# Spectral block with a gated MLP: the second token block transposed by VectorE and DMA, where TensorE did it

## The chip, the core and the metric

The kernel runs on one core of a Trainium2 chip. The core has five engines with queues of their own, which run in order and wait for each other by semaphores: TensorE (PE in the profile; its weight loads are PEld), VectorE (DVE), ScalarE (ACT), GpSimd (POOL) and SyncE (SP), which here issues nearly all DMAs. TensorE writes to PSUM, eight banks of 128 partitions x 2 KB; the other tensors lie in SBUF, 128 partitions wide. The metric is the device time of one execution in microseconds, the median of three runs.

## The reference

```python
x = A_x                                                  # 1 x 2048 tokens x 640 features, float32
X = rfft2(layernorm(x)) * (w_r + 1j * w_i)
h = x + irfft2(X)
n = layernorm(h)
out = h + ((n @ w_gate) * (n @ w_up)) @ w_down           # 640 -> 1728 -> 640
```

## The kernel before

The first part, up to about 180 us, does the Fourier filter as matrix products and adds its result to x; from there on the tiles X[0] to X[15] hold h, 128 tokens x 640 features each. The rest is the gated MLP, in two blocks of 1024 tokens (blk 0: X[0..7], blk 1: X[8..15]); a block has two halves sb of 512 tokens.

Products need n transposed, features on the partitions. The tile xt[:, sb, k, l] holds, for half sb and feature block k of five, 128 features x 512 tokens, split in a high part (l = 0, rounded to the fast product type) and a low part (l = 1, what is left). Every product is done as three matmuls, high x high, high x low and low x high.

Hidden features come in 14 chunks of 128. Chunks 12 and 13 are made by plain products, gate and up (gu), and multiplied by gate_parts. Chunks 0 to 11 go through strassen: gate and up, feature blocks 0-1 and 2-3 and the two token halves make a 2 x 2 block product, done by the Winograd form in six steps with seven product groups (the fifth feature block is added to them). The form needs sums of n's blocks: t1 = n(1, k) - n(0, k), t2 = n(1, k+2) - t1, t3 = t2 - n(0, k) and t4 = n(0, k+2) - t2, each split in high and low as well; t4 takes the place of xt[:, 1, 0:2]. The chunks go in pairs p; the order of the pairs in a block is 6, 0, 1, 2, 3, 4, 5, where 6 stands for chunks 12 and 13. A pair's down products are done during the next pair, by groups that strassen starts at its slots 1 to 7 (at(n)): slots for the even chunk and slots for the odd one. Into the same slots the lists side put other work. The last pair's down products, one per token tile (down), stand at the change of blocks: 12 matmuls into two of four PSUM banks (tag d), then two additions to X on VectorE and the tile's store.

Everything is emitted in the order in which the program is written, and each engine's queue follows it. What sets the work around the change:

- prep(c): the weights of chunk c lie raw in stage; ScalarE and GpSimd split them (copies), form the weights' own sums (sums) and split those (high, low). load_raw then loads the next chunk's into stage, on SP's queue.
- The pool work has eight buffers (wk) for everything short-lived: ScalarE's copies h0, c22 and h1 of each chunk, of which an even chunk's are kept until the odd one, the raw down weights (draw), normalised tiles. A new tile takes a buffer that is free, and its first writer waits for the old one's last reader, a DMA too.
- fill holds the 32 small operations that make the layernorm factors of X[8..15]; one is popped behind each group of down products, the rest at chunk 11.
- At the end of block 0 (chunk 11) ScalarE normalises X[8..15] (L646), and TensorE starts to transpose them: turn_mm makes four 128 x 128 transposes of one token tile into a PSUM bank of tag e (L658), turn_hi copies them to xt and, for tiles 0 to 3, to bt, turn_lo makes the low part and, for tiles 4 to 7, the first two sums (L681, L682). fifth does the fifth feature block of four tiles at once (L689). These alternate with the eight down products. Behind them stand the plain products gu of chunks 13 and 12, and beside them t12, t_rest and t34 finish the sums.

Of the kernel before, what the change touches and what calls it, by code (L numbers as in the profile page):

```python
# [16 lines left out]
P = 128  # L17
# [4 lines left out]
NC = 14  # L22
# [16 lines left out]
def f32(ap):  # L39
    return ap.bitcast(F32)  # L40
# [29 lines left out]
def tile_spectral_glu(ctx: ExitStack, tc: tile.TileContext, x, wf, wgu, wlast, wdown, wdlast,  # L70
# [595 lines left out]
    def turn_hi(t):  # L666
        hi, pk = turned(t, 0)
        act(hi, pk, AF.Copy)
        if t % 8 == 0:
            TJ["b"] = home("dA", [P, 4, 4, P], "bt")  # L670
        if t % 8 < 4:
            act(TJ["b"][:, t % 4], pk[:, 0:4], AF.Copy)

    def turn_lo(t):
        lo, pk = turned(t, 1)
# [39 lines left out]
    def transp(t):  # L715
        turn_mm(t)
        turn_hi(t)
        turn_lo(t)
# [228 lines left out]
    def strassen(c, blk, ahead, downs, side):  # L947
# [84 lines left out]
        elif odd:  # L1032
            hi_of(oa, 5)
            lo_of(oa, 5)

    order = [6, 0, 1, 2, 3, 4, 5]
    steps = [(blk, p) for blk in range(2) for p in order]
    prev = None
    for n, (blk, p) in enumerate(steps):
        if p == 6:  # L1040
            if blk == 0:
                load_raw(0)
                copies, sums, high, low = prep(0, blk, nc.vector)
# [24 lines left out]
                wdn = load_d(p)  # L1068
            else:
                copies, sums, high, low = prep(0, blk)  # L1070
                js = [4, 5, 6, 7, 0, 1, 2, 3]
                for j in range(8):
                    if j:
                        transp(8 + j)
                    else:
                        turn_lo(8)
                    if j % 4 == 3:
                        fifth(range(5 + j, 9 + j))
                    if j >= 1:
                        down(*prev, js[j - 1], True)  # L1080
                    if j == 3:
                        copies()
                        sums()
                    if j == 5:
                        high()
                        low()
                down(*prev, js[7], True)
                wdn = load_d(p)
                gu(NC - 1, 0)
                gate_parts(NC - 1, 0)()  # L1090
                gu(NC - 2, 0)
                TJ["12"] = home("qr", [P, 2, 2, 2, 512], "t12", F32R)
                t1s = [t12(j) for j in range(4)]
                late = gate_parts(NC - 2, 0)
                for j in range(4):
                    t1s[j][0]()
                    t_rest(j)
                late()
                gu(NC - 1, 1)
                for j in range(4):  # L1100
                    t1s[j][1]()
                late = gate_parts(NC - 1, 1)
                issue(wdn)
                hi, lo = t34(0)
                hi()
                late()
            gu(NC - 2, 1)
            g = gate_parts(NC - 2, 1, wdn[0] if blk == 0 else ())
            rest = t34(1)
            rest[0]()  # L1110
            g()
            lo()
            rest[1]()
# [12 lines left out]
        if prev[1] == 6:  # L1126
            js = [[0], [1, 2], [3], [4, 5], [6, 7]]
            slots[0] = {n: [lambda j=j, prev=prev: down(*prev, j) for j in k] for n, k in enumerate(js, 3)}
        else:
            fs = down_products(*prev, (0, 1)) + down_products(*prev, (2, 3))  # L1130
            slots[0] = dict(zip(range(1, 8), fs))
            slots[1] = dict(zip((1, 2, 7) if p == 5 else (2, 3, 4), fs[7:]))
        for ci in range(2):
            c = 2 * p + ci
            side = {n: [] for n in range(8)}
            ahead = None
            if c < 11:
                ahead = prep(c + 1, blk)
                if c < 10:
                    side[6 if ci else 7].append(lambda c=c: load_raw(c + 2))  # L1140
            if p == 5:
                if ci == 0:
                    side[3].append(lambda wdn=wdn: issue(wdn))
                else:
                    side[4].append(lambda: (split(HELD["a11"], 0), split(HELD["a21"], 3)))
            elif ci == 0:
                for n, i in ((3, 0), (6, 1), (7, 2)):
                    side[n].append(wdn[i])
            else:
                def rest(wdn=wdn, ahead=ahead):  # L1150
                    split(HELD["a11"], 0)
                    ahead[2]()
                    ahead[3]()
                    wdn[3]()
                    split(HELD["s3"], 5)
                    wdn[4]()

                side[4].append(rest)
            if c == 11 and blk == 0:
                pop(len(fill))  # L1160
                dj = load_direct(1, [wk([P, D], "draw"), stage[:, 0:640], stage[:, 640:1280]])
                side[1] += [lambda: issue(dj[0]), lambda: issue(dj[1]), lambda: load_raw(0)]

                def norms(ks):
                    for k in ks:
                        if k == 0:
                            TJ["z"] = home("qr", [P, 6, D], "zt")
                        normalise(8 + k, TJ["z"][:, k] if k < 6 else wk([P, D], "z"))

                for n, ks in ((3, (0, 1, 2)), (5, (3, 4)), (6, (5, 6)), (7, (7,))):  # L1170
                    side[n].append(lambda ks=ks: norms(ks))
                side[7] += [lambda: turn_mm(8), lambda: turn_hi(8)]
            strassen(c, blk, ahead, slots[ci], side)
        prev = (blk, p)
    for j in (4, 5, 6, 0, 1, 2, 3, 7):
# [132 lines left out]
```

## Time and profile before

| | |
|---|---|
| median of 3 runs | 691.53 us (691.51 to 691.61) |
| the profiled execution | 692.1 us |
| its span in the trace | 690.3 us |
| TensorE busy, share of the span | 98% |
| VectorE, ScalarE, GpSimd | 69%, 46%, 56% |
| chunks 8 to 11 of block 0 | about 336 to 411 us of the span |
| down products and transposes at the change of blocks | 411 to 430 us |
| the four plain products behind them | 430 to 450 us |

A row of the timeline has the start and the length in us, the engine, the line, the operation, what it writes and reads, the shape, a count where equal instructions follow each other, and in brackets how long the engine stood idle before it and what released it. A row of the groups has the count, the busy time, the mean ns of one, and the idle time before them. PE's matmuls are pipelined: the pace is read from the starts, best of the weight loads. A row of a DMA queue has its packets, its MB and the time that they took as a share of 16 engines' span; a row of DMA issues has the count, the size of one and the median us from issue to landing.

### The profile page before, as it was taken

How to read it: one execution, taken by the hardware profiler on the slowest of the kernel's cores; microseconds unless marked ns; L12 is line 12 of the kernel's file. 1: busy time of each engine (PE TensorE's matmuls, PEld its weight loads, DVE VectorE, ACT ScalarE, POOL GpSimd, SP SyncE). 2: the span in 40 equal slices, each digit the busy share in tenths (PEclk: the TensorE clock that was granted, in tenths of full speed). 3: DMA queues.
4: the chain of work that ended last, by engine and by line, in shares of the span. 5: the costliest groups of instructions: out<-in, count | busy, mean ns of one | idle time of the engine just before them, and what ended most of it. 6: DMA issues, size and time to landing. Idle time of an engine off the chain costs nothing.

```text
span 690.3 us, 10276 instructions
## 1 busy us (share of the span) xinstructions
PE 679.8 (98%) x3784; PEld 602.3 (87%) x3784; DVE 478.3 (69%) x980; ACT 318.8 (46%) x615; POOL 383.4 (56%) x364
## 2 busy tenths in 40 slices
PE   8999999999999999999999999999999999999998
PEld 8989998887888888888888889888888888888887
DVE  7968887897963858586867648553757575765654
ACT  6976665375533434252525184342625252525320
POOL 3101113321097887878787644086887878797610
PEclk9999999999999999999999999999999999999999
DMA  9516763001120212121212112401212121212004
GB/s 334 195 56 213 236 206 118 1 1 38 43 78 35 76 39 77 39 76 39 77 38 96 39 39 114 153 1 38 78 39 77 38 77 39 76 39 74 4 1 153
DMA packets 21075, 55.07 MB, mean 80 GB/s; under 512 B 2336, under 2 KB 7200, under 8 KB 21024
## 3 DMA queue, kind: packets, MB, share of 16 engines
q1 hardware_dynamic: 20304, 52.53, 22.2%
q0 software_dynamic: 288, 1.48, 0.6%
q8 instruction: 30, 0.49, 0.3%
q10 hardware_dynamic: 432, 0.39, 0.2%
q14 instruction: 21, 0.17, 0.1%
HBM read 49.16 MB, written 5.24 MB: 79 GB/s over the span
## 4 chain that ended last, share of the span: by engine, by line
PE 81%; DVE 11%; ACT 4%; POOL 2%; issue 1%; ACTq 0%; DVEq 0%
PE e L109 41%; PE d L109 23%; PE re L109 2%; PE im L109 2%; PE u L413 2%; PE im L455 2%; PE eo L109 2%; PE im L241 2%; DVE ht L941 1%; PE re L282 1%; POOL wst L836 1%; PE ir L455 1%; PE y L109 1%; ACT wst L847 1%; DVE x L631 1%
## 5 line engine op out<-in xcount | busy, mean ns | idle before, releaser
L109 PE MATMUL e<-xt,wst 128*128 128x512 f32 x864 | 213.1, 390 | 0.0
L109 PEld LDWEIGHTS e<-xt,wst 128*128 128x128 f32 x864 | 159.9, 188 | 30.7
L922 DVE TENSOR_TENSOR x<-d,x 128x320 f32<-128x320 f32 x280 | 123.7, 484 | 49.4 <-PE d L109 44.9
L109 PE MATMUL d<-wd,ht 128*128 128x320 f32 x832 | 145.1, 309 | 0.3 <-DVE x L922 0.2
L109 PEld LDWEIGHTS d<-wd,ht 128*128 128x128 f32 x832 | 130.8, 188 | 8.1 <-DVE x L897 0.6
L836 POOL TENSOR_TENSOR wst<-raw,wst 128x1024 fp32r<-128x1024 f32 x23 | 56.8, 2472 | 70.9 <-ACT wst L835 68.1
L109 PE MATMUL e<-t,wst 128*128 128x512 f32 x288 | 74.0, 392 | 0.2 <-ACT h L977 0.2
L109 PE MATMUL d<-wt,ht 128*128 128x320 f32 x360 | 69.6, 311 | 0.4 <-DVE x L922 0.4
L852 POOL TENSOR_TENSOR wst<-raw,wst 128x896 fp32r<-128x896 f32 (+1 forms) x46 | 65.1, 1438 | 0.2 <-ACT wst L847 0.2
L109 PEld LDWEIGHTS e<-t,wst 128*128 128x128 f32 x288 | 52.7, 188 | 10.0 <-ACT h L977 0.6
L109 PEld LDWEIGHTS d<-wt,ht 128*128 128x128 f32 x360 | 57.3, 188 | 3.3 <-issue 0.9
L992 DVE TENSOR_TENSOR e<-e,h 128x512 f32<-128x512 f32 x24 | 16.8, 700 | 47.0 <-PE e L109 34.1
L977 ACT ACTIVATE h<-e 128x512 f32<-128x512 f32 x24 | 14.3, 595 | 74.7 <-PE e L109 74.7
L847 ACT ACTIVATE wst<-raw 128x896 fp32r<-128x896 f32 (+1 forms) x48 | 30.2, 678 | 35.0 <-POOL raw L841 34.2
L484 POOL CAST qr<-bits 1x128 fp32r<-1x128 f32 x15 | 4.2, 280 | 71.4 <-DVE qr L488 71.4
L938 ACT ACTIVATE ht<-e 128x512 fp32r<-128x512 f32 x44 | 26.3, 597 | 37.3 <-DVE e L996 14.2
L109 PE MATMUL e<-xt,wdir 128*128 128x512 f32 x180 | 42.1, 392 | 0.2 <-DVE ht L791 0.2
L109 PEld LDWEIGHTS e<-xt,wdir 128*128 128x128 f32 x180 | 33.5, 188 | 7.5 <-issue 0.6
L580 ACT ACTIVATE wd<-draw 128x320 fp32r<-128x320 f32 (+1 forms) x30 | 15.6, 555 | 50.3 <-POOL draw L589 50.0
L941 DVE TENSOR_TENSOR ht<-e,ht 128x512 fp32r<-128x512 f32 x54 | 37.0, 685 | 2.0 <-ACT ht L938 1.6
L560 POOL TENSOR_TENSOR wd<-draw,wd 128x640 fp32r<-128x640 f32 x8 | 12.4, 1569 | 46.1 <-ACT wd L559 46.1
L897 DVE TENSOR_TENSOR x<-d,x 128x320 f32<-128x320 f32 x62 | 27.4, 485 | 14.5 <-PE d L109 14.5
(207 smaller groups left out, 1256.8 us busy)
## 6 DMA issues: line engine op xcount, KB each, us to landing
raw<-in_wgu_dram SPq DMA_DIRECT2D x24, 640.0 KB, 4.0
wts<-in_wf_dram SPq DMA_DIRECT2D x16, 644.0 KB, 4.0
draw<-in_wdown_dram SPq DMA_DIRECT2D x24, 320.0 KB, 4.6
x<-in_x_dram SPq DMA_DIRECT2D x15, 320.5 KB, 5.8
out_dram<-x SPq DMA_DIRECT2D x15, 320.0 KB, 2.2
bits<-in_mm_dram SPq DMA_DIRECT2D x32, 128.0 KB, 3.9
raw<-in_wgu_dram SPq DMA_DIRECT2D x4, 320.0 KB, 4.3
draw<-in_wdlast_dram SPq DMA_DIRECT2D x4, 320.0 KB, 4.2
```

The lines of the kernel that those rows point to most:

```text
L109: nc.tensor.matmul(o, l, r, start=start, stop=stop, skip_group_check=True)
L455: nc.tensor.matmul(out, y[:, h, a:b], inv(g, h), start=n == 0, stop=n == len(ys) - 1)
L580: act(o[:, 0, a:a + n], src, AF.Copy)
L836: ptt(wa[:, 1], stage[:, 0:1024], f32(wa[:, 0]), op=OP.subtract)
L847: act(ws[:, 0, o:o + b - a], stage[:, a:b], AF.Copy)
L852: ptt(ws[:, 1, o:o + b - a], stage[:, a:b], f32(ws[:, 0, o:o + b - a]), op=OP.subtract)
L897: tt(xv, ps[b][:, 0:320], xv, op=OP.add)
L922: tt(xv, o, xv, op=OP.add)
L938: act(hop[:, a, 0], src, AF.Copy)
L941: engine.tensor_tensor(hop[:, a, 1], src, f32(hop[:, a, 0]), op=OP.subtract)
L977: act(h0, oa, AF.Copy)
L992: tt(ob, ob, h1, op=OP.add)
```

## The change

In block 0, X[8..11] are normalised and turned in chunk 8, X[12..15] in chunk 10. A turn (flip) is one VectorE instruction that transposes each 32 x 32 block of the 128 x 640 tile in its place, then four DMAs, one for each 32 partitions, that write it to a buffer zfar in HBM so that a row of zfar holds one feature and all 1024 tokens; each DMA writes 640 runs of 32 elements. In chunk 11, fetch reads zfar back by 16 DMAs into five tiles of 128 features x 512 tokens for each half (z), in the places of the last pair's down weights and two wk buffers. All 40 transposes of this block go. At the change of blocks ScalarE makes xt's high parts from z and copies z to PSUM, VectorE makes the low parts, one behind each down product; the sums t1 to t4 are formed in two PSUM banks of tag d between the plain products, from z and from each other.

Moved with it: what is left in fill is popped before chunk 8; for p = 5 the odd chunk's down groups stand at slots 2, 3 and 4 in place of 1, 2 and 7, in both blocks; the split of the direct weights (issue(dj)) and the load of chunk 0's weights go from slot 1 to slot 6 of chunk 11.

```diff
+    far = ctx.enter_context(tc.tile_pool(name="far", bufs=1, space=bass.MemoryType.DRAM))
...
-        if t % 8 == 0:
+        if t == 0:
             TJ["b"] = home("dA", [P, 4, 4, P], "bt")
...
+    zfar = far.tile([32, 5, 4, 1024], F32, name="zfar")
...
                 copies, sums, high, low = prep(0, blk)
-                js = [4, 5, 6, 7, 0, 1, 2, 3]
-                for j in range(8):
-                    if j:
-                        transp(8 + j)
-                    else:
-                        turn_lo(8)
-                    if j % 4 == 3:
-                        fifth(range(5 + j, 9 + j))
-                    if j >= 1:
-                        down(*prev, js[j - 1], True)
...
+                z = [[TJ[sb][k] for k in range(5)] for sb in range(2)]
+                t1s = home("qr", [P, 2, 2, 2, 512], "t12", F32R)
+                TJ["12"] = t1s
+
+                def hi(sb, ks):
+                    for k in ks:
+                        act(xt[:, sb, k, 0], z[sb][k], AF.Copy)
+
+                def copied(sb, k, bank=single):
+                    o = bank()
+                    act(o, z[sb][k], AF.Copy)
+                    return o
+
+                def lo(sb, k, o):
+                    tt(xt[:, sb, k, 1], o, f32(xt[:, sb, k, 0]), op=OP.subtract)
...
+                hi(0, range(2))
+                held = [copied(0, 0), copied(0, 1)]
+                hi(0, range(2, 5))
+                work_of = [(0, 0), (0, 1), (0, 2), (0, 3), (0, 4), (1, 2), (1, 3), (1, 4)]
+                for i, j in enumerate((4, 5, 6, 7, 0, 1, 2, 3)):
+                    down(*prev, j, True)
+                    lo(*work_of[i], held[i])
+                    if i < 6:
+                        held.append(copied(*work_of[i + 2]))
+                    if i == 1:
+                        hi(1, (2, 3, 4))
+                    if i == 3:
                         copies()
                         sums()
+                    if i == 4:
+                        hi(1, (0, 1))
+                    if i == 6:
                         high()
                         low()
...
+                pb = [copied(1, k, lane) for k in range(2)]
+                late = gate_parts(NC - 1, 0)
+                for k in range(2):
+                    lo(1, k, pb[k])
+                late()
+                for k in range(2):
+                    tt(pb[k], pb[k], z[0][k], op=OP.subtract)
...
-            slots[1] = dict(zip((1, 2, 7) if p == 5 else (2, 3, 4), fs[7:]))
+            slots[1] = dict(zip((2, 3, 4), fs[7:]))
...
             if c == 11 and blk == 0:
-                pop(len(fill))
                 dj = load_direct(1, [wk([P, D], "draw"), stage[:, 0:640], stage[:, 640:1280]])
-                side[1] += [lambda: issue(dj[0]), lambda: issue(dj[1]), lambda: load_raw(0)]
...
+                side[6] += [lambda: issue(dj[0]), lambda: issue(dj[1]), lambda: load_raw(0)]
+
+                def fetch():
+                    z = home("dA", [P, 5, 512], "z0")
+                    TJ[0] = [z[:, k] for k in range(5)]
+                    y = home("dC", [P, 3, 512], "z1")
+                    ys = [wk([P, 1, 512], "z1") for _ in range(2)]
+                    TJ[1] = [y[:, 0], y[:, 1], y[:, 2], ys[0][:, 0], ys[1][:, 0]]
+                    for sb, k, o in ((0, 0, z), (1, 0, y), (1, 3, ys[0]), (1, 4, ys[1])):
+                        for q in range(4):
+                            nc.sync.dma_start(o[32 * q:32 * q + 32],
+                                              zfar[:, k:k + o.shape[1], q, 512 * sb:512 * sb + 512])
+
+                side[5].append(fetch)
+            if blk == 0 and c in (8, 10):
+                def flip(k):
+                    r = wk([P, D], "zr")
+                    nc.vector.transpose(r, Z[8 + k])
+                    o = zfar.rearrange("a k q n -> a (k q) n")
+                    for i in range(4):
+                        nc.sync.dma_start(o[:, :, P * k + 32 * i:P * k + 32 * i + 32],
+                                          r[32 * i:32 * i + 32].rearrange("a (g b) -> a g b", b=32))
+
+                if c == 8:
+                    pop(len(fill))
+                for i in range(4):
+                    k = 4 * (c // 2 - 4) + i
+                    side[(1, 3, 5, 6)[i]].append(lambda k=k: normalise(8 + k, wk([P, D], "z")))
+                    side[(2, 4, 6, 7)[i]].append(lambda k=k: flip(k))
```

How the instructions stand on the engines (the changed kernel's lines are one or a few higher). On TensorE at the end of chunk 11 and the change of blocks, before; wd and wt are down weights, ht the gated hidden features, ident the unit matrix of the transposes, zt and z the normalised tokens, wdir the weights of chunks 12 and 13:

```order
L109 MATMUL e<-xt,wst 128x512 x18
L109 MATMUL d<-wd,ht 128x320 x3
L109 MATMUL d<-wt,ht 128x320 x6
L658 MATMUL e<-ident,zt 128x128 x8
L109 MATMUL d<-wd,ht 128x320 x12
L658 MATMUL e<-ident,zt 128x128 x4
L109 MATMUL d<-wd,ht 128x320 x12
L658 MATMUL e<-ident,zt 128x128 x4
L689 MATMUL e<-ident,zt 128x128 x4
L109 MATMUL d<-wd,ht 128x320 x12
```

And TensorE there now:

```order
L110 MATMUL d<-wd,ht 128x320 x3
L110 MATMUL d<-wt,ht 128x320 x6
L110 MATMUL e<-ht,wst 128x512 x6
L110 MATMUL e<-xt,wst 128x512 x18
L110 MATMUL d<-wd,ht 128x320 x96
L110 MATMUL e<-xt,wdir 128x512 x90
```

The group of nine down matmuls that stood behind chunk 11 now stands before its last four product groups, and the eight down products follow each other without a transpose.

On VectorE at the same place, from the low part of chunk 11's hidden features (ht) on, before; x is a token tile of the result:

```order
L941 TENSOR_TENSOR ht<-e,ht 128x512
L676 TENSOR_TENSOR xt<-e,xt 128x4x128 x2
L897 TENSOR_TENSOR x_70<-d,x_70 128x320 x2
L676 TENSOR_TENSOR xt<-e,xt 128x4x128
L897 TENSOR_TENSOR x_71<-d,x_71 128x320 x2
L676 TENSOR_TENSOR xt<-e,xt 128x4x128
L692 TENSOR_TENSOR xt<-e,xt 128x512
L897 TENSOR_TENSOR x_72<-d,x_72 128x320 x2
```

And VectorE now:

```order
L942 TENSOR_TENSOR ht<-e,ht 128x512
L898 TENSOR_TENSOR x_72<-d,x_72 128x320 x2
L1087 TENSOR_TENSOR xt<-e,xt 128x512
L898 TENSOR_TENSOR x_73<-d,x_73 128x320 x2
L1087 TENSOR_TENSOR xt<-e,xt 128x512
L898 TENSOR_TENSOR x_74<-d,x_74 128x320 x2
```

Each down product's two additions are followed by one low part of a whole feature block (L1087), which reads the PSUM copy and the high part that ScalarE has made.

On SP's queue from chunk 8 to the change of blocks, before; draw are raw down weights and, with raw, the raw weights of chunks 12 and 13:

```order
L824 DMA raw<-in_wgu_dram 128x1280 x2
L558 DMA draw<-in_wdown_dram 128x640 x2
L558 DMA draw<-in_wlast_dram 128x640
L558 DMA raw<-in_wgu_dram 128x640 x2
L824 DMA raw<-in_wgu_dram 128x1280
```

And SP now:

```order
L1230 DMA zfar<-zr 640x1x32 x12
L825 DMA raw<-in_wgu_dram 128x1280
L1230 DMA zfar<-zr 640x1x32 x4
L825 DMA raw<-in_wgu_dram 128x1280
L559 DMA draw<-in_wdown_dram 128x640 x2
L1230 DMA zfar<-zr 640x1x32 x16
L559 DMA draw<-in_wlast_dram 128x640
L559 DMA raw<-in_wgu_dram 128x640 x2
L1220 DMA z_3935<-zfar 32x5x512 x4
L1220 DMA z_3936<-zfar 32x3x512 x4
L1220 DMA z_3937<-zfar 32x512 x4
L1220 DMA z_3938<-zfar 32x512 x4
```

The loads of the weights of chunks 10 and 11 (raw) now stand behind the stores of three turns and of a fourth, and the load of chunk 0's weights for the next block comes behind all loads from zfar.

More of the change, by code (lines that the diff above doesn't have):

```diff
@@ L1099, in tile_spectral_glu @@
+                gu(NC - 2, 0)
+                late = [t12(0, k) for k in range(2)]
+                for f in late:
+                    f()
+                for k in range(2):
+                    tt(pb[k], z[1][k + 2], pb[k], op=OP.subtract)
+                late = [t12(1, k) for k in range(2)]
+                g = gate_parts(NC - 2, 0)
+                for f in (late[0], g, late[1]):
+                    f()
                 gu(NC - 1, 1)
[L1100 to L1101 removed]
+                pd = [lane() for _ in range(2)]
@@ L1102, in tile_spectral_glu @@
+                for k in range(2):
+                    tt(pd[k], z[0][k], pb[k], op=OP.subtract)
+                    tt(pb[k], z[0][k + 2], pb[k], op=OP.subtract)
                 late = gate_parts(NC - 1, 1)
+                late = [t34(0, 0), late, t34(0, 1)]
+                for f in late:
+                    f()
                 issue(wdn)
-                hi, lo = t34(0)
-                hi()
-                late()
             gu(NC - 2, 1)
             g = gate_parts(NC - 2, 1, wdn[0] if blk == 0 else ())
-            rest = t34(1)
@@ L1110, in tile_spectral_glu @@
[L1110 to L1113, printed above, removed]
+            if blk:
+                g()
+                for f in [t34(1, k) for k in range(2)]:
+                    f()
+            else:
+                rest = t34(1)
+                rest[0]()
+                g()
+                lo()
+                rest[1]()
             if blk == 0:
```

34 lines of the change are left out of this document (13 added, 21 removed).

## The prediction

> **What bounds the kernel now.** I read first the page's engine line, its slices and the totals of the chain that ended last.
>
> ```profile
> PE 679.8 (98%) x3784; PEld 602.3 (87%) x3784; DVE 478.3 (69%) x980; ACT 318.8 (46%) x615; POOL 383.4 (56%) x364
> ...
> PE   8999999999999999999999999999999999999998
> ...
> PE 81%; DVE 11%; ACT 4%; POOL 2%; issue 1%; ACTq 0%; DVEq 0%
> ```
>
> TensorE is busy in every slice and makes up 81% of the chain, so a TensorE instruction that goes is worth its own time, unless another engine then holds TensorE up. Next I read the busy time of the stretches that the change touches: the first block's chunk 8 (with the end of 7), the change of blocks, and the four gate products behind it.
>
> ```profile
> core 0: us, PE busy (x) PEld busy (x) DVE busy (x) ACT busy (x) POOL busy (x), PEclk, DMA share, GB/s
> 340.40:359.60 19.20, 19.00 (x101) 16.63 (x100) 15.01 (x29) 5.33 (x10) 15.95 (x15) 1.00 0.10 35
> 411.10:430.20 19.10, 19.02 (x138) 18.51 (x137) 15.37 (x34) 10.88 (x20) 8.44 (x7) 1.00 0.27 104
> 430.20:450.50 20.30, 20.30 (x92) 16.81 (x91) 10.70 (x19) 7.98 (x14) 1.62 (x2) 1.00 0.39 130
> ```
>
> The clock is granted in full (1.00) and TensorE has almost no gap in any of them. VectorE has 4 us free in the first two and 10 us in the last; the DMA engines are used to 10 to 39%.
>
> **Transposes removed.** The timeline at the change of blocks, weight loads (PEld) only, because their starts show the pace:
>
> ```profile
> 411.04 0.94 PEld L658 LDWEIGHTS e<-ident,zt 128*128 128x128 f32 x8
> 411.95 1.77 PEld L109 LDWEIGHTS d<-wd,ht 128*128 128x128 f32 x12
> 413.68 0.51 PEld L658 LDWEIGHTS e<-ident,zt 128*128 128x128 f32 x4
> 414.15 1.76 PEld L109 LDWEIGHTS d<-wd,ht 128*128 128x128 f32 x12
> ...
> 430.08 20.31 PEld L109 LDWEIGHTS e<-xt,wdir 128*128 128x128 f32 x90
> ```
> ```profile
> PEld d L109 <- DVE x L897: 0.6, 2, 0.3
> ```
>
> From the first transpose (411.04) to the first gate product (430.08) are 19.04 us. In them stand 8 down products of 12 matmuls, 1.77 us each, 14.16 us, and 40 transposes at some 0.11 us (0.47 for four, 413.68 to 414.15), 4.3 us; the rest is the 0.6 us in which the loads waited for VectorE's additions. With the transposes gone the stretch can shrink to 14.16: **-4.9 us**, if operands and PSUM banks come in time.
>
> **What feeds the second block instead.** For each of 10 feature blocks ScalarE makes the high part (10 copies) and a PSUM copy (10 more), and VectorE one low part. Eight of these low parts alternate with the additions of the down products. Rows of the stretch that has such work now, and ScalarE's normalise:
>
> ```profile
> L676 DVE TENSOR_TENSOR xt<-e,xt 128x512 fp32r<-128x512 f32 x8 | 5.4, 687 | 2.0 <-ACT xt L668 1.8
> L897 DVE TENSOR_TENSOR x<-d,x 128x320 f32<-128x320 f32 x12 | 5.3, 481 | 0.0
> L668 ACT ACTIVATE xt<-e 128x512 fp32r<-128x512 f32 x8 | 4.6, 592 | 2.8 <-PE e L658 2.7
> L646 ACT ACTIVATE z<-x,b,r 128x640 f32<-128x640 f32 x2 | 1.7, 910 | 0.0
> ```
>
> Per down product VectorE has 2 x 0.48 + 0.69 = 1.65 us against TensorE's 1.77: it keeps up, with little to spare. ScalarE has 18 such operations of 0.59 (10.6 us) and two weight splits in 14.2 us, also close. The L681 and L682 operations go; the sums move behind the down products as 8 VectorE operations of 0.69 (5.5 us) where 10 us are free, two low parts beside them (1.4), with four t1/t2 low parts as before. So the gate stretch stays at 20.3: 0.
>
> **The 32x32 turns in chunks 8 and 10.** Eight on VectorE, eight normalises (0.91 us) moved up on ScalarE, which is busy 5.33 of 19.2 us there. Rows of chunk 8, and one wide SBUF operation from the next block:
>
> ```profile
> 342.00 2.41 POOL L836 TENSOR_TENSOR wst<-raw,wst 128x1024 fp32r<-128x1024 f32 x1 [4.45 <-ACT wst L835]
> 342.32 2.11 DVE L198 SCALAR_TENSOR_TENSOR r<-w,r 128x8 f32<-128x8 f32 x1
> 344.36 1.47 DVE L922 TENSOR_TENSOR x<-d,x 128x320 f32<-128x320 f32 x3
> 344.89 0.70 PE L109 MATMUL d<-wd,ht 128*128 128x320 f32 x3 [0.20 <-DVE x L922]
> ...
> 454.09 1.22 DVE L707 TENSOR_TENSOR xt<-bt,xt 128x1024 fp32r<-128x1024 f32 x1
> ```
>
> No row shows a turn. Between 0.69 for 512 elements and 1.22 for 1024, 640 elements take about 0.82 us (estimate). Behind each turn stand additions that free the four d banks. The trace prices such a block: L198, eight elements from SBUF, lasted 2.11 us, ending with GpSimd's L836, and TensorE then lost 0.20. So a turn costs TensorE between 0 and 0.2, eight together 0 to 1.6; as a turn is nearer to the additions' own length than to 2.11, I take 0.4. L198 itself moves ahead of the chunk, where GpSimd idles (4.45 before 342.00): -0.2.
>
> **The stores to HBM and what they are queued before.** Each turn is stored by four DMAs of 640 runs of 128 B on SP's queue. Three turns (12 DMAs) stand ahead of the load of chunk 10's weights, one more turn behind it. Buffers tie this to compute: in chunk 9 ScalarE's c22 takes the buffer of turn 3 and its second copy that of turn 4, so each waits for that turn's four stores; turns 3 and 4 wait for the stores of 1 and 2, which have 8 us.
>
> ```profile
> 353.15 18.68 SPq L824 DMA_DIRECT2D raw<-in_wgu_dram  x2
> 354.38 1.28 DVE L922 TENSOR_TENSOR x<-d,x 128x320 f32<-128x320 f32 x3
> ...
> 357.76 1.48 DVE L922 TENSOR_TENSOR x<-d,x 128x320 f32<-128x320 f32 x3
> ...
> 360.35 1.05 ACT L835 ACTIVATE wst<-raw 128x1024 fp32r<-128x1024 f32 x1
> 361.89 0.60 ACT L985 ACTIVATE c<-e 128x512 f32<-128x512 f32 x1 [0.49 <-PE e L109]
> 364.65 0.60 ACT L989 ACTIVATE h<-e 128x512 f32<-128x512 f32 x1 [2.16 <-PE e L109]
> 365.27 2.23 PE L109 MATMUL e<-xt,wst 128*128 128x512 f32 x9
> 368.65 1.55 PE L109 MATMUL e<-ht,wst 128*128 128x512 f32 x6
> ```
> ```profile
> q1 hardware_dynamic: 20304, 52.53, 22.2%
> q10 hardware_dynamic: 432, 0.39, 0.2%
> raw<-in_wgu_dram SPq DMA_DIRECT2D x24, 640.0 KB, 4.0
> out_dram<-x SPq DMA_DIRECT2D x15, 320.0 KB, 2.2
> ```
>
> Turn 3 ends at 355.7 + 0.8 = 356.5; four issues of 0.33 to 0.45 follow, then the load (358.2 instead of 353.15), which lands 4.0 later at 362.2; the split at 360.35 slips to 362.2 and c22 to about 363.9. TensorE needs c22 by 365.27: no loss. Call F the time that a turn's packets hold the 16 engines, 160 each. From 358.2 - 1.7 + 1.4 (out_dram's 2.2 less its data) F counts in full above 1.7, and the slack of 1.4 is gone at F = 3.2. A mean packet was 22.2% x 16 x 690.3 / 20304 = 121 ns for 2.59 KB on q1 and 51 ns for 0.90 KB on q10; the line through both gives 19 ns for 128 B, F = 3.0. The upper bound is 51 ns a packet, F = 8.2; the lower is issue alone, 1.7. I take 3.0, on the line through rows, so 0 loss; the bounds make the rival below.
>
> [...]
>
> **The loads back.** Sixteen DMAs, each to 32 partitions, wait for the last products that read the old tiles; for that the last down group of chunk 11 moves from slot 7 to slot 4.
>
> ```profile
> 395.37 1.55 PE L109 MATMUL e<-xt,wst 128*128 128x512 f32 x6
> 402.65 0.60 ACT L989 ACTIVATE h<-e 128x512 f32<-128x512 f32 x1 [1.66 <-PE e L109]
> 405.79 4.24 PE L109 MATMUL e<-xt,wst 128*128 128x512 f32 x18
> 410.07 0.70 DVE L1017 TENSOR_TENSOR e<-e,h 128x512 f32<-128x512 f32 x1 [0.75 <-PE e L109]
> ```
>
> In the new order 30 products of 0.226 (20.31 / 90) and 24 down matmuls of 0.1475 come first: 395.37 + 6.78 + 3.54 = 405.7. Chunk 11 ends at 411.1 as before, so the moved group itself costs 0. The first half (1280 KB) lands like two raw loads in line: 4.0 + 640 KB more (1.9 at q1's pace) = 411.6. When must it? TensorE's fourth down product (411.1 + 3 x 1.77 = 416.4) needs the additions of the second, which stand behind the first low part; back from there over 0.96 + 0.69 and three or four copies of 0.59 it is about 413. In time by 1.4 at full pace; at half pace the data part (3.8) doubles and it is 2.4 late, of which about 2.0 reaches TensorE. All rows go to 128 partitions, so neither is shown: bounds 0 and 2.0, and between them I take 0.9.
>
> **The sum.** -4.9 - 0.2 + 0.4 + 0 + 0.9 = -3.8 us on the profiled execution (span 690.3, time 692.1), which is 0.57 above the median of 691.53; on the median that makes **687.7 us**. A measurement of this kernel tells some 0.2% (1.4 us) from no change.
>
> **Rivals.**
> 1. *The stores hold up chunks 9 and 11, slower.* Place: ScalarE's split, c22 and second copy in chunk 9, and the second copy of chunk 11 (402.65), which waits for turn 8. For it: 20480 packets of 128 B, as many as q1 carried in all, and issues that may grow with their 640 runs (5 x 0.33 = 1.65 each, F = 6.6). Against: the line through the rows. At F = 6.6 c22 is 3.4 late; turn 4's packets come behind the load, 2.2 more; turns 5 to 8 queue up and turn 8 is 5.8 late: 11.4 us, 699 us. It decides from F about 5.3 (33 ns a packet).
> 2. *The loads back run at half pace, faster by less.* 2.0 instead of 0.9: 688.8, and up to 690 if the second half delays ScalarE again. [...] At a quarter of the pace the first half lands at 423, the second near 438: some 11 us, 699.
> 3. *Turns held like L198.* 2.11 instead of 0.82 each, 1.6 instead of 0.4 on TensorE, and c22 of chunk 9 another 1 later: 689 to 690.5.
> 4. *The change frees nothing:* VectorE's 1.65 beside 1.77 slips past TensorE's pace through waits on ScalarE, 0.3 to 0.6 a product: 690 to 692.
>
> **How the numbers follow.** Forecast 0.42, half pace 0.20, slow stores or quarter pace 0.26, held turns 0.07, nothing freed 0.05. Faster: 0.42 + 0.20 + 0.04 of held turns = 0.66; same: 0.03 + 0.05 = 0.08; slower 0.26. The forecast's own range is 686 to 689. The range for 8 in 10 starts below its best case (no cost at all: 691.5 - 5.1 = 686.4) at 685.8 and ends at rival 1's 699.
>
> **What would show it.** Right: at the change of blocks 96 down loads in a row, 14 to 16 us, no waits for additions; c22 of chunk 9 near 364; turns near 0.8 us. Wrong: TensorE idle in chunks 9 or 11 behind ScalarE and that behind DMA (stores), or a gap before the fourth down product (loads back), or turns of 2 us beside GpSimd.

## The result, and the profile after

The changed kernel takes 690.76 us (median of 22 runs, 690.45 to 691.91), the kernel before, run beside it, 691.65 us. The ratio is 0.9986, with a 95% interval of 0.9979 to 0.9993: 0.9 us faster, where 3.8 were forecast. The profiled execution took 691.03 us with a span of 689.3, against 690.3 before.

From the page after, the engine line and the totals of the chain that ended last:

```profile
PE 676.4 (98%) x3744; PEld 597.8 (87%) x3744; DVE 483.7 (70%) x985; ACT 322.8 (47%) x623; POOL 383.6 (56%) x364
...
PE 76%; DVE 12%; ACT 5%; POOL 2%; DMA 2%; issue 2%; SPq 0%; DVEq 0%; ACTq 0%
```

The 40 transposes are gone (3744 instead of 3784 matmuls). But TensorE's share of the chain fell from 81 to 76%, and DMA, which was not in it, has 2%: somewhere TensorE now waits for others. The timeline of the weight loads after shows where (start, length, then in brackets the idle time ahead and what ended it):

```profile
411.11 5.40 PEld L110 LDWEIGHTS d<-wd,ht 128*128 128x128 f32 x36
417.35 0.19 PEld L110 LDWEIGHTS d<-wd,ht 128*128 128x128 f32 x1 [0.84 <-DVE x L898]
417.74 8.65 PEld L110 LDWEIGHTS d<-wd,ht 128*128 128x128 f32 x59 [0.21 <-DVE x L898]
426.36 20.31 PEld L110 LDWEIGHTS e<-xt,wdir 128*128 128x128 f32 x90
446.70 1.32 PEld L110 LDWEIGHTS e<-xt,wst 128*128 128x128 f32 x6
449.22 1.22 PEld L110 LDWEIGHTS e<-t,wst 128*128 128x128 f32 x6 [1.20 <-ACT wd L560]
450.48 0.65 PEld L110 LDWEIGHTS e<-xt,wst 128*128 128x128 f32 x3
452.78 1.22 PEld L110 LDWEIGHTS e<-t,wst 128*128 128x128 f32 x6 [1.65 <-ACT h L978]
454.05 1.58 PEld L110 LDWEIGHTS d<-wd,ht 128*128 128x128 f32 x10
```

and the same place of the kernel before, from chunk 0 of the second block on:

```profile
450.43 1.32 PEld L109 LDWEIGHTS e<-xt,wst 128*128 128x128 f32 x6
451.79 1.32 PEld L109 LDWEIGHTS e<-t,wst 128*128 128x128 f32 x6
453.15 0.64 PEld L109 LDWEIGHTS e<-xt,wst 128*128 128x128 f32 x3
453.83 1.32 PEld L109 LDWEIGHTS e<-t,wst 128*128 128x128 f32 x6
455.19 1.58 PEld L109 LDWEIGHTS d<-wd,ht 128*128 128x128 f32 x10
```

From the starts of these rows, stage by stage:

| stage | before | after | difference |
|---|---|---|---|
| up to the end of chunk 11 (first row behind it) | 411.04 | 411.11 | +0.07 |
| down products at the change of blocks | 19.04 | 15.25 | -3.79 |
| the four gate products | 20.35 | 20.34 | 0 |
| chunk 0, up to its first down product | 4.76 | 7.35 | +2.59 |
| from there to the end | 235.1 | 235.25 | +0.14 |

The stages that the prediction priced came out nearly as priced. What it did not price is chunk 0 of the second block, some 35 us behind the loads back: two waits there eat 2.6 of the 3.8 us that the change of blocks became shorter.

The chain of waits of the changed kernel leads from there straight back to the loads from HBM (start, length, engine, what; shortened at the dots):

```profile
409.55 8.37 DMA z<-zfar
...
418.34 5.77 DMA raw<-in_wgu_dram
...
424.19 1.07 ACT wst L836
...
425.33 2.44 POOL wst L837
...
429.74 0.74 POOL raw L842
...
430.50 0.85 ACT wst L848
...
431.76 1.02 ACT d L1083 x2
...
432.79 0.61 ACT u L789
...
433.42 0.69 DVE e L790
...
449.93 0.71 DVE e L786
...
452.24 0.50 ACT h L978
...
452.78 1.65 PE e L110 x6
```

Read from the top: the sixteen loads back (z) are on SP's queue ahead of the load of chunk 0's weights (raw), which is issued at 418.34. ScalarE splits those weights at 424.19 and then must wait for GpSimd's sums of them, until 430.50 (L848). Behind that wait, in ScalarE's own queue, stand two copies of z that VectorE needs and gate (13,0)'s copy u (L789, 432.79). VectorE was idle until u came (5.38 us) and then worked through its list up to 452, with three waits of 0.67 to 1.15 us for copies of ScalarE, which had waited for VectorE's results itself; the copy h that TensorE waits for in chunk 0 comes at the end of that list. From u to this h it takes 19.45 us (432.79 to 452.24). The two queues:

```profile
430.50 1.26 ACT L848 ACTIVATE wst<-raw 128x896 fp32r<-128x896 f32 x2 [3.20 <-POOL raw L842]
431.67 1.10 ACT L1083 ACTIVATE d<-z 128x512 f32<-128x512 f32 x2
432.79 0.60 ACT L789 ACTIVATE u<-e 64x512 f32<-64x512 f32 x1
```
```profile
433.42 0.69 DVE L790 TENSOR_TENSOR e<-e,u 64x512 f32<-64x512 f32 x1 [5.38 <-ACT u L789]
```

and u in the kernel before, where ScalarE had nothing to do ahead of it:

```profile
433.91 0.59 ACT L788 ACTIVATE u<-e 64x512 f32<-64x512 f32 x1 [6.79 <-PE e L109]
```

Before, u came 3.83 us behind the first gate product (433.91 - 430.08), as soon as the product that it copies was done. After, it comes 6.43 us behind it (432.79 - 426.36): 2.60 late, and chunk 0 loses 2.59.

### The profile page after: what moved, and what is told of

The parts are those of the page before. It is cut to its first block, busy times and chain, and to the rows that moved or that the text cites. A ratio compares the mean times of both kernels' runs of the same rounds, so it can differ in the third digit from the quotient of the medians.

```text
span 689.3 us, 10294 instructions
## 1 busy us (share of the span) xinstructions
PE 676.4 (98%) x3744; PEld 597.8 (87%) x3744; DVE 483.7 (70%) x985; ACT 322.8 (47%) x623; POOL 383.6 (56%) x364
## 4 chain that ended last, share of the span: by engine, by line
PE 76%; DVE 12%; ACT 5%; POOL 2%; DMA 2%; issue 2%; SPq 0%; DVEq 0%; ACTq 0%
PE e L110 37%; PE d L110 23%; PE re L110 2%; PE im L110 2%; PE u L414 2%; PE im L456 2%; PE eo L110 2%; PE im L242 2%; PE re L283 1%; DMA z<-zfar 1%; DVE ht L942 1%; POOL wst L837 1%; PE ir L456 1%; DMA raw<-in_wgu_dram 1%; PE y L110 1%
## 5 line engine op out<-in xcount | busy, mean ns | idle before, releaser
L110 PE MATMUL d<-wd,ht 128*128 128x320 f32 x832 | 143.5, 309 | 0.6 <-DVE x L898 0.6
L837 POOL TENSOR_TENSOR wst<-raw,wst 128x1024 fp32r<-128x1024 f32 x23 | 55.4, 2411 | 69.4 <-ACT wst L836 69.4
L848 ACT ACTIVATE wst<-raw 128x896 fp32r<-128x896 f32 (+1 forms) x48 | 30.2, 677 | 33.4 <-POOL raw L842 32.6
L110 PE MATMUL e<-ht,wst 128*128 128x512 f32 x144 | 37.1, 392 | 0.0
```

Of the source, the lines that this page charges most:

```text
L110: nc.tensor.matmul(o, l, r, start=start, stop=stop, skip_group_check=True)
L837: ptt(wa[:, 1], stage[:, 0:1024], f32(wa[:, 0]), op=OP.subtract)
L848: act(ws[:, 0, o:o + b - a], stage[:, a:b], AF.Copy)
```

## Experiments

Three theories of the 2.6 us were tried. **Theory 1**: the load of chunk 0's weights is late behind the loads back, and ScalarE's wait for it holds u back. **Theory 2**: VectorE, which now makes all sums, has too much work in the gate stretch, whenever it starts. **Theory 3**: ScalarE's own order at the end of the stretch, the split of the down weights ahead of the last u, makes h late. A fourth question is why the loads back are slow. All edits are to the changed kernel; all times are compared with 690.76 (after) and 691.7 (before, 691.65 to 691.72 beside these runs).

### The wait moved behind u

```diff
-                    if i == 6:
-                        high()
-                        low()
...
                 for k in range(2):
                     lo(1, k, pb[k])
                 late()
+                high()
+                low()
```

> The high and low parts of chunk 0's weight sums move on ScalarE and GpSimd from between the last down products to behind gate (13,0). Theory 1 (late weights): the load of chunk 0's weights stands behind the sixteen loads on SP's queue, GpSimd's sums of it end 3.2 us late, and the two copies of xt's last feature blocks and gate (13,0)'s copy u stand behind ScalarE's wait for them. Without that wait u(13,0) comes at about 430 instead of 432.8, VectorE starts its sums some 3 us earlier, and chunk 0's waits of 0.81 and 1.65 us go: 2.3 to 2.6 us off the changed kernel's 690.8, 688.2 to 688.5. Theory 2 (VectorE is full): its work in the gate stretch, not its start, makes it late; no more than 0.5 us off, 690.3 or more. Theory 3 (ScalarE's order at the end of the stretch, the splits of the down weights ahead of the last u): 0.5 us off at most.

Measured: 687.52 us (687.34 to 687.81), ratio to before 0.9940 (0.9928 to 0.9953). ScalarE and the weight loads of this kernel:

```profile
429.36 0.59 ACT L789 ACTIVATE u<-e 64x512 f32<-64x512 f32 x1 [1.30 <-PE e L110]
```
```profile
425.53 20.31 PEld L110 LDWEIGHTS e<-xt,wdir 128*128 128x128 f32 x90
445.88 1.32 PEld L110 LDWEIGHTS e<-xt,wst 128*128 128x128 f32 x6
...
450.64 1.58 PEld L110 LDWEIGHTS d<-wd,ht 128*128 128x128 f32 x10
```

u waits for its product alone, 3.83 us behind the first gate product as before, and chunk 0 is back at 4.76 us (450.64 - 445.88). The instructions are the same ones; only the place of two helpers in the queues of ScalarE and GpSimd differs. So theory 1's last link holds, and theory 2 in its plain form falls: VectorE does the same work in time if it starts in time. The kernel is some 0.7 us better than expected; in its profile chunk 11 ended 0.4 us earlier and the gap at 417 was 0.4 shorter, which differs from execution to execution: in after, this kernel and the next two, which are the same up to there, the down products start between 410.42 and 411.11. From u to chunk 0's h it takes 19.31 us (429.36 to 448.67), as after: the same list with the same three waits, begun earlier.

### ScalarE's splits earlier

```diff
+                issue(wdn)
                 late = gate_parts(NC - 1, 1)
                 late = [t34(0, 0), late, t34(0, 1)]
                 for f in late:
                     f()
-                issue(wdn)
```

> ScalarE splits the down weights before gate (13,1) instead of behind it, where it waits 3.7 us for VectorE anyway. Theory 1: the first copy of chunk 0 (h0) comes 1.25 us earlier, but ob's bank is still freed by VectorE at 449.1, so the first wait of 0.81 to 1.2 us stays: 0.4 to 1.2 us off, 689.6 to 690.4. Theory 2: the same or less. Theory 3: the whole 2.6 us go, 688.2.

Measured: 690.45 us (690.13 to 691.38), 0.3 less than after, with ranges that overlap. Chunk 0 took 7.63 us in the profile (445.56 to 453.19) against 7.35: nothing gained there. Theory 3, by which the whole 2.6 us would go, falls. So does a detail of theory 1 as it was put: h did not come 1.25 earlier, because ScalarE then waited 1.84 us for VectorE (447.38 to 449.81). The first wait of chunk 0 stayed as well, 1.15 us against 1.20, though after the profile had named these splits as what ended it (ACT wd L560). VectorE's queue, not ScalarE's, carries the delay from u to chunk 0.

### Less work in VectorE's queue

```diff
-                pd = [lane() for _ in range(2)]
-                for k in range(2):
-                    tt(pd[k], z[0][k], pb[k], op=OP.subtract)
-                    tt(pb[k], z[0][k + 2], pb[k], op=OP.subtract)
```

> From the changed kernel, four of VectorE's subtractions of 0.6 us between gates (13,0) and (13,1) are left out (the last two operand sums of each half keep their old values, so this kernel leaves out part of the computation). The loads and the late u(13,0) stay. If the delay of u(13,0) (2.6 us against the kernel before, counted from the first gate product) reaches chunk 0 through VectorE's queue, 2.4 us less work there takes back nearly as much: 0.2 to 0.6 us lost in chunk 0 instead of 2.6, 688.2 to 688.8. If it reaches chunk 0 through ScalarE's queue alone, the time stays at 690.3 or more.

The kernel leaves out the last four operand sums; the parts of t3 and t4 are then made from older values. Measured: 688.30 us (688.07 to 688.49), within the range expected. u is even later in its profile, 7.10 us behind the first gate product (432.40 - 425.30), 3.27 more than it need be; without 2.4 us of VectorE's work 0.87 of that should reach chunk 0, and 0.89 does: 5.65 us from 445.64 to 451.29 (the 0.2 to 0.6 expected there went by a u 2.6 late). Theory 2 is thus half right: VectorE has not too much work, but no slack at all behind u.

### The loads back to 128 partitions

```diff
-    zfar = far.tile([32, 5, 4, 1024], F32, name="zfar")
+    zfar = far.tile([4, 32, 5, 1024], F32, name="zfar")
...
-                        for q in range(4):
-                            nc.sync.dma_start(o[32 * q:32 * q + 32],
-                                              zfar[:, k:k + o.shape[1], q, 512 * sb:512 * sb + 512])
+                        nc.sync.dma_start(o, zfar[:, :, k:k + o.shape[1], 512 * sb:512 * sb + 512]
+                                          .rearrange("q a k n -> (q a) k n"))
```

> The intermediate in HBM is laid out with its quarter outermost, so that each load back is one DMA to 128 partitions: 4 DMAs instead of 16, same bytes, stores of the same 128 B runs. If the pace of the loads is set by their 32 partitions: packets of 2048 B fall from 158 ns to some 85 to 100, the first half lands near 412 instead of 414.5, TensorE's gap of 1.05 us before the fourth down product goes, and by theory 1 the load of chunk 0's weights, no longer behind sixteen issues, starts at about 415 (when GpSimd has read the buffer) instead of 418.3, which gives back up to 1.7 of the 2.6 us more: 688.0 to 689.8. If reading HBM or the other traffic sets the pace, packets stay near 158 ns, the gap stays, and only the earlier start of the weights' load counts: 689.1 to 690.8.

Measured: 687.10 us (686.92 to 687.30), ratio to before 0.9933 (0.9920 to 0.9947): better than the best case expected. The chain of waits of this kernel around the change of blocks:

```profile
405.67 5.46 PE e L110 x24
411.13 14.07 PE d L110 x96
425.21 25.20 PE e L110 x111
450.41 1.46 PE d L110 x10
```

TensorE alone, from chunk 11 to the down products behind chunk 0, with no gap. The packets tell why (durations from the traces' records of single DMA packets): the 1280 packets of 2048 B in the loads back lasted 158 ns in the median after, 84 ns here, and 84 was about the fastest of after as well. In the windows from 405.50 to 412.00, while the first half loads, the last two numbers are the DMA engines' busy share and GB/s; after, then here:

```profile
405.50:412.00 6.50, 6.50 (x33) 5.54 (x32) 4.35 (x9) 2.48 (x4) 1.83 (x3) 1.00 0.86 180
```
```profile
405.50:412.00 6.50, 6.50 (x34) 5.54 (x33) 4.23 (x8) 2.57 (x5) 2.14 (x2) 1.00 0.90 305
```

The engines are about equally busy and move 180 or 305 GB/s: a packet to 32 partitions just takes longer. On SP's queue the loads take up less time too:

```profile
404.82 2.47 SPq L1219 DMA_DIRECT2D z<-zfar  x4
414.55 0.33 SPq L825 DMA_DIRECT2D raw<-in_wgu_dram  x1
```

where after the sixteen issues lasted from 405.18 to 418.24. So the weights' load goes out as soon as GpSimd has read the old contents of its buffer (414.5), u comes 3.83 us behind the first gate product, and chunk 0 takes 4.77 us.

### The late weights put back

To the wide loads, the load of chunk 0's weights is made late again:

```diff
-                side[6] += [lambda: issue(dj[0]), lambda: issue(dj[1]), lambda: load_raw(0)]
+                side[6] += [lambda: issue(dj[0]), lambda: issue(dj[1])]
...
                     down(*prev, j, True)
+                    if i == 2:
+                        load_raw(0)
```

> The four wide loads stay, and only the cause that theory 1 names is put back: the load of chunk 0's weights is issued behind the third out store of block 0 (near 419.5) instead of at 414.5. Theory 1: it lands near 424, ScalarE's high parts come near 430 again, the copies and u(13,0) behind them near 432, and chunk 0 of the second block loses 2 to 2.6 us again: 689.1 to 689.8, against 687.1 with the wide loads alone. Theory 2 (VectorE has too much work in the gate stretch, and the wide loads relieved it otherwise): no more than 0.4 us: 687.5 or less.

Measured: 689.49 us (688.80 to 690.79), 2.4 us above the wide loads alone. ScalarE here:

```profile
422.15 1.06 ACT L836 ACTIVATE wst<-raw 128x1024 fp32r<-128x1024 f32 x1 [2.59 <-DMA raw<-in_wgu_dram]
...
428.45 1.26 ACT L848 ACTIVATE wst<-raw 128x896 fp32r<-128x896 f32 x2 [3.19 <-POOL raw L842]
429.62 1.11 ACT L1083 ACTIVATE d<-z 128x512 f32<-128x512 f32 x2
430.75 0.60 ACT L789 ACTIVATE u<-e 64x512 f32<-64x512 f32 x1
```

u comes 6.04 us behind the first gate product (424.71), 2.21 late; chunk 0 takes 6.94 us, 2.18 more than it need. The loads at full pace stayed and the late weights alone brought the loss back: theory 1 is shown from both sides.

### The weights' load on another queue

```diff
-                side[6] += [lambda: issue(dj[0]), lambda: issue(dj[1]), lambda: load_raw(0)]
+                side[6] += [lambda: issue(dj[0]), lambda: issue(dj[1]),
+                            lambda: nc.gpsimd.dma_start(stage[:, 0:1280], wgu[0])]
```

> The sixteen loads back stay as they are; only the load of chunk 0's weights goes on GpSimd's queue instead of SP's, so that it no longer stands behind them and starts near 415 instead of 418.3. Theory 1: ScalarE's high copy of it moves up until the copies ahead of it in its own queue end (about 422.5 instead of 424.2), the wait behind GpSimd's sums ends 1.7 us earlier, and chunk 0 loses about 1 instead of 2.6; but the same bytes now compete with the second half of the loads back, which may give 0.5 back: 689.0 to 690.2. Theory 2: no change, 690.5 to 691.

Measured: 690.86 us (690.17 to 691.32), no change, where theory 1 as I had put it gave 689.0 to 690.2. The load goes out 3.4 us earlier (414.96), but the second half of the loads back, under way at the same time, now comes later (ScalarE's copy that waits for it starts at 422.69 instead of 420.85), and ScalarE stands before that instead:

```profile
422.69 0.63 ACT L1079 ACTIVATE xt<-z 128x512 fp32r<-128x512 f32 x1 [3.01 <-DMA z<-zfar]
...
424.27 1.04 ACT L836 ACTIVATE wst<-raw 128x1024 fp32r<-128x1024 f32 x1
```

The split of the weights starts at 424.27 instead of 424.19. TensorE now stands 1.04 us before the last down product too, and the gate products start at 426.96; chunk 0 loses 2.06 in place of 2.59. I read this so: while the loads run at half pace, the queue decides who waits and the pace decides how long.

### Width or number of the loads

Two more forms of the loads, both with the layout in HBM of the wide loads: 10 DMAs to 128 partitions (one for each feature block), and 8 DMAs to 64 partitions.

```diff
+                        for i in range(o.shape[1]):
+                            nc.sync.dma_start(o[:, i], zfar[:, :, k + i, 512 * sb:512 * sb + 512]
+                                              .rearrange("q a n -> (q a) n"))
```

> Each load back goes to 128 partitions as in the wide loads, but one DMA for each feature block: 10 DMAs instead of 4 (or 16 narrow ones), so that number and width come apart. If width alone sets the pace: packets of 2048 B stay at 84 ns, no gap before the fourth down product, 686.9 to 687.5. If the number of outstanding DMAs counts too: SP is held up behind the eighth, the load of chunk 0's weights starts later than 414.5, and the time lies between 687.5 and 689.

```diff
+                        for h in range(2):
+                            nc.sync.dma_start(o[64 * h:64 * h + 64],
+                                              zfar[2 * h:2 * h + 2, :, k:k + o.shape[1], 512 * sb:512 * sb + 512]
+                                              .rearrange("q a k n -> (q a) k n"))
```

> The loads back as 8 DMAs to 64 partitions each (0 to 63, 64 to 127), 2048 B a packet as before. If the pace goes with the number of partitions, 64 are twice 32: packets near 84 ns and 687.0 to 687.5. [...]

| loads back | median packet of 2048 B | SP's queue, first to last issue | us |
|---|---|---|---|
| 16, to 32 partitions (after) | 158 ns | 13.06 us | 690.76 |
| 8, to 64 partitions | 159 ns | 5.44 us | 689.42 (689.14 to 689.98) |
| 10, to 128 partitions | 84 ns | 6.66 us | 687.13 (686.84 to 687.54) |
| 4, to 128 partitions | 84 ns | 2.47 us | 687.10 (686.92 to 687.30) |

Ten DMAs are as good as four, so up to ten their number does not matter. Twice the partitions bring nothing to a packet, though the layout in HBM is that of the wide loads, so that it is not the layout that made those fast; the window of the 64-partition kernel reads

```profile
405.50:412.00 6.50, 6.50 (x33) 5.54 (x33) 4.35 (x9) 2.48 (x4) 1.83 (x3) 1.00 0.79 175
```

175 GB/s, as with 32. What the eight loads bring is a shorter queue on SP (the weights' load at 414.94): u is 1.33 late and chunk 0 loses 1.32. The idea that the pace grows in step with the number of partitions falls: 159 ns a packet with 64, 158 with 32, 84 with 128. What makes 64 partitions no faster than 32, no run here shows.

### The stores doubled

```diff
+    zfar2 = far.tile([32, 5, 4, 1024], F32, name="zfar2")
...
+                        nc.sync.dma_start(o2[:, :, P * k + 32 * i:P * k + 32 * i + 32],
+                                          r[32 * i:32 * i + 32].rearrange("a (g b) -> a g b", b=32))
```

> Each turned piece is stored a second time, into an HBM tensor that nobody reads. The prediction's slack: a turn's packets may hold the engines 3.2 us before chunk 9 is late; measured they hold them 160 x 13 ns = 2.1, doubled 4.2, and SP issues 8 instead of 4 DMAs a turn at 0.64 us each. The load of chunk 10's weights then goes out at about 361.6 instead of 359.0 and ScalarE's c22 of chunk 9 runs near 367 instead of 364.6, 1.5 to 2 us after TensorE needs it; with turns 4 to 8 the loss is 2 to 4 us: 692.8 to 694.8. If other buffers give more slack than the prediction saw, 691.3 or less.

Measured: 697.84 us (697.76 to 698.69), 7.1 us slower than after, more than expected. The places in chunk 9 are the ones that the first rival named:

```profile
361.34 0.58 SPq L825 DMA_DIRECT2D raw<-in_wgu_dram  x1
```
```profile
367.55 1.90 PEld L110 LDWEIGHTS e<-xt,wst 128*128 128x128 f32 x9 [2.95 <-ACT c L986]
...
372.39 1.23 PEld L110 LDWEIGHTS e<-ht,wst 128*128 128x128 f32 x6 [1.47 <-ACT h L990]
```

Chunks 8 to 11 lose 3.7 us. The rest was not expected: SP issues the doubled stores of chunk 10 one by one at 0.64 us, so the loads back start at 410.40 instead of 405.18, and the down products at the change of blocks lose 3.95 more. The run doubles the packets and the issues together and does not tell which of the two costs how much.

### Everything together

Wide loads, the weights on GpSimd's queue, the wait behind u, the earlier splits, and the load of chunk 10's weights ahead of turn 3's stores.

> Everything together: wide loads, the weights' load on GpSimd's queue, the weight sums' high and low parts behind gate (13,0), the down weights' splits before gate (13,1), and the load of chunk 10's weights ahead of turn 3's stores. With the wide loads alone TensorE waits only 0.28 us in chunk 9 (for c22, behind those stores) from there to the second block's first down products, and by theory 1 the other edits take away waits that are already gone: 0.2 to 0.4 us off 687.1, 686.6 to 687.0. Theories 2 and 3 would have the earlier start and the earlier splits bring up to 1 us more: 686.0.

Measured: 686.90 us (686.73 to 687.08), ratio to before 0.9932 (0.9920 to 0.9945). It is 0.2 us from the wide loads alone, although two of its edits bring 3.2 and 3.7 us each by themselves: they take away one and the same loss. The fastest kernels here, this and the wide loads, are 4.6 to 4.8 us faster than the kernel before.

### One number for all of them

How late u is against the 3.83 us that its product needs, and what chunk 0 loses against the 4.76 us of before, in the profile of each kernel:

| kernel | u late | chunk 0 loses |
|---|---|---|
| before; wait behind u; wide loads; ten loads; everything together | 0 | 0 |
| stores doubled | 1.27 | 1.25 |
| 64 partitions | 1.33 | 1.32 |
| weights on another queue | 2.08 | 2.06 |
| wide loads, weights late | 2.21 | 2.18 |
| after | 2.60 | 2.59 |
| splits earlier | 3.09 | 2.87 |
| four sums (2.4 us) left out | 3.27 | 0.89 |

Except where VectorE's work itself was cut, chunk 0 loses what u is late, to within 0.22 us. The gap before the fourth down product belongs to the same account: after, the gap is 1.05 and u 2.60 late, with the splits earlier 0.59 and 3.09, 3.65 and 3.68 us in sum. u's own time is set by the loads in both, so a longer gap only moves the gate products nearer to it. Accordingly the chain of waits above runs from the loads to u and not through the gap.

## Why the prediction came out as it did

**Transposes, -4.9: right.** With the wide loads the stretch from the first down product to the first gate product is 14.15 us (410.75 to 424.90), where 14.16 was worked out. After, it is 15.25, by the gap of the loads back.

**Turns, +0.4, and L198, -0.2: the two cost nothing.** No turn was held by GpSimd:

```profile
L1227 DVE STREAM_TRANSPOSE zr<-z 128x640 f32<-128x640 f32 x8 | 6.7, 834 | 0.0
```

834 ns against 0.82 us estimated. Chunks 8 to 11 together end 0.07 later, and 0.23 of waiting in chunk 9 belongs to the stores, so the +0.2 forecast for the two is not there. The third rival falls.

**Stores, 0: right but for 0.23.** The load of chunk 10's weights went out at 359.00 (358.2 forecast) and c22 ran at 364.62 (363.9), because an issue of 640 runs takes 0.64 us on SP's queue, not 0.33 to 0.45:

```profile
359.00 0.58 SPq L825 DMA_DIRECT2D raw<-in_wgu_dram  x1
```
```profile
363.65 1.06 ACT L836 ACTIVATE wst<-raw 128x1024 fp32r<-128x1024 f32 x1 [3.13 <-DMA raw<-in_wgu_dram]
364.62 0.58 ACT L986 ACTIVATE c<-e 128x512 f32<-128x512 f32 x1
```

TensorE lost 0.23 there. The packets themselves were cheaper than thought, 13 ns in the median against 19, F = 2.1 instead of 3.0. The first rival had the right place and the wrong size: doubling the stores, packets and issues, brings it to life.

**Loads back, +0.9: the right place, and a price that is right by luck.** The gap before the fourth down product is 0.84 + 0.21 = 1.05 us. But 0.9 was taken as a middle between full and half pace, and the loads did run at half pace, 158 ns a packet against 84. ScalarE's first copy of z starts at 414.53, where the working gave 411.6 at full pace, 415.4 at half pace and about 413 as the time by which it was needed. The gap is no fixed price either: it was 0.55 to 0.63 in the first three kernels of the experiments, which have the same sixteen loads, and where nothing else was done about u it was the later for it. What the narrow loads cost as a whole is the 3.7 us that the wide loads give back (690.76 - 687.10). The half pace from which the upper bound of 2.0 and the second rival were worked out was an assumption that no row of before shows, as all of them go to 128 partitions; the runs showed it, with 158 ns, and a gap of 1.05 us in place of the 2.0.

**The step that failed: "So the gate stretch stays at 20.3: 0".** The gate products did stay at 20.34 us. But the step counted VectorE's work (5.5 + 1.4 us) against the 10 us that it had free in this stretch, and ScalarE's weight splits as work alone, without asking when either can start and who needs the last piece. After, the free time lies ahead of u (5.38 us idle up to 433.42) and is lost; from there on VectorE has no slack, so each microsecond by which u is late is paid by TensorE in chunk 0: 2.59 us where 0 was put. That u would be late could be read too: the change puts the load of chunk 0's weights behind the sixteen loads back on SP's queue, from 402.91 before to 418.34 (the row before is below), and ScalarE has the splits of those weights ahead of its last copies and of u. The prediction followed what the stores are queued before, and did not do the same for the loads back.

```profile
402.91 0.33 SPq L824 DMA_DIRECT2D raw<-in_wgu_dram  x1
```

**The second rival came true in its pace, not in its path.** It priced half pace at 2.0 us before the fourth down product, where 1.05 were lost, and "up to 690 if the second half delays ScalarE again". ScalarE was delayed, but by the load of weights behind the second half, and the loss came in chunk 0; that the 690.76 lies near its 690 is luck in part. The fourth rival, that the change frees nothing at the down products, falls: VectorE's 1.65 beside 1.77 us keeps up, as the 14.15 us show. With the loads at full pace the rest of the sum holds: 687.7 less the 0.9 is 686.8, and the wide loads took 687.10.

## What to carry to other kernels

When a transfer is put into a queue, follow every transfer behind it to its reader, and that reader's queue to the next engine; a load that nobody seems to wait for can be the head of a chain that ends 35 us later, as here. Free time of an engine counts only if it lies behind the moment at which its work can start. And write loads so that one DMA covers all 128 partitions: here 2048 B took 84 ns so, and 158 to 159 with 32 or 64. It was a matter of the layout in HBM and cost nothing in the stores, whose last four issues took 2.62 us with the narrow loads' layout and 2.64 with the other.

## What the runs showed of the hardware

- A DMA to 32 partitions, or to partitions 0 to 63 or 64 to 127, moves 2048 B packets at 158 to 159 ns in the median, one to 128 partitions at 84: 175 to 180 GB/s against 305 in the same window.
- A DMA of 640 runs of 128 B takes 0.64 us in the median to issue on SP's queue, one of a whole weight tile 0.33 (at 402.91 before, 374.81 after) and 0.58 right behind the stores (359.00 after). The packets of 128 B last 13 ns in the median, less than the 19 ns that the prediction read from longer ones; 128 B in 13 ns are 0.4 of the pace of 2048 B in 84.
- VectorE's transpose of the 32 x 32 blocks of a 128 x 640 float32 tile takes 0.83 us in all eight turns, beside the 0.82 estimated from two additions, also while GpSimd works (the turns at 349.45 and 355.42).
